# Top-k attention with a gated feed-forward: pairs of slots begin at slot 13, single blocks for x, two buffers for loaded q and k, values copied between the softmax's two functions

## The chip, the core and the metric

The kernel runs on one core of one Trainium2 chip. The metric is the device time of one execution in microseconds (us). The program works on five engines: TensorE (PE in the profile, its weight loads PEld), VectorE (DVE), ScalarE (ACT), GpSimd (POOL) and SyncE (SP), which issues nearly all DMA. Each engine takes its own instructions strictly in the order in which they are written.

## The reference

```python
# attention: q, k, v are (8, 8, 576, 64); top_k = 32
scores = scale * np.matmul(q, k.transpose(0, 1, 3, 2))
kth = np.partition(scores, -top_k, axis=-1)[..., -top_k:-top_k + 1]
scores = np.where(scores >= kth, scores, -1000000000.0)
attn = np.exp(scores - np.max(scores, axis=-1, keepdims=True))
attn = attn / (np.sum(attn, axis=-1, keepdims=True) + 1e-09)
x = np.matmul(attn, v)            # then (B,H,S,D) -> (B*S, H*D) = (4608, 512)
# feed-forward: w_in (512, 2048), w_out (2048, 512)
h = x @ w_in
g = h * (1.0 / (1.0 + np.exp(-1.702 * h)))
out = g @ w_out
```

Each row keeps the 32 largest of its 576 scores.

## The kernel before, in words

**Slots.** The unit of attention is a slot: 128 rows for two heads, thus 2 x 128 rows of 576 scores. A batch has four blocks of 128 rows and a tail of 64, times four pairs of heads: 16 full slots and two tail slots, 18 in all (`PER`), and 144 slots for the eight batches (`N`). In each batch the two tail slots are the 13th and 14th.

**What a slot goes through.** `scores` (PE, L282) fills PSUM, `copy_scores` (ACT, L294) brings it to SBUF. A top-k search on DVE finds the 32nd largest value. `exponentials` (ACT) runs two functions over the row: a Prelu that throws everything below the cut far down (L388) and an Exp whose sums fall out beside it (L391). The probabilities are transposed, and the values matmul (PE, L495 or L530) makes a 64-row piece of x for each head. When all four pairs of heads of a block are there, the block of x (128 tokens x 512) is put on the list `ready`. A quarter of the first feed-forward matmul for one block is `hidden` (L580, written H below), the quarter of the second is `project` (L628, P). A block takes four H and four P; there are 36 blocks, so 144 of each. Between them lie a tanh on ACT (L597, and a copy L600) and the gate on POOL (L609, L610), or on DVE in the first slots (L612).

**Two forms of slots.** Slots 0 to 11 (`SETTLED`) run one at a time in `slot(n)`. Their search (`topk`) runs over all 576 columns. The probabilities are transposed by PE matmuls against a diagonal matrix `by` with the inverse sums (L440, L443; `by` is made on POOL, L404, after `divide` on DVE has waited for the sums). From slot 12 on `two_slots(n)` runs slots n and n + 1 together. Its search (`topk_of_pairs`) first takes the greater and the lesser of column j and column j + 288: `pair_up` (DVE L323 for the greater, POOL L326 and L327 for the lesser), a slot ahead. It takes 32 values of the greater half and 16 of the lesser with MAX8 and MATCH_REPLACE8 over 288 columns (L337, L340), merges the two lists (L344) and takes the least (L347). The probabilities are transposed by DMA: `split` (ACT L462) separates the halves of each word, a DMA writes them to DRAM (L464), and a transposing DMA (L470) brings them back as `pt`. Inverse sums of a pair of slots are spread out on POOL (`wide`, L425), turned by PE (L519), copied with the values from PSUM to SBUF by ACT (`x`, L908), and multiplied on POOL into the block of x (`x_of`, L544).

**The order inside a pair.** The order is written by hand. For pair n: loads of slot n; bounds and `exponentials(n - 1)`, `split`; search n; H; P; tanh; `prepare_by_dma`; the turned sums of slots n - 3 and n - 2; scores n + 2 and their copy; values of n - 3 and n - 2; the transposing DMAs; scores n + 3; loads of slot n + 1; bounds and `exponentials(n)`; the copy `x` and `x_of`; `split(n)`; H; copy of scores n + 3; tanh; `prepare_by_dma` of slot n + 1; P; the copy of a finished output block (`ob`, L634); search n + 1. On PE this reads: H, P, turned sums, S(n + 2), values, S(n + 3), H, P.

**q and k of the next batch.** `load` (SP L184, L187: six DMAs for q and k of one pair of heads) fills `qk_l`, `prepare_by_dma` splits it (ACT L240, `halves`), writes it to DRAM (L244 to L249) and transposes it back (L253). Two tables say in which slot this happens, counted from the first slot of the batch: `FETCH` and `READY`, with tables of their own for batch 1 (`FETCH_1`, `READY_1`); `VALUES` does so for v.

**Buffers.** The pool `loads` has one buffer, `xtp` three of 128 x 4 x 2 x 128 (two blocks of x each), `ptp` and `prp` two each (`prp` holds the probabilities and `halves`), `ps_s` room for one slot's scores.

Of the kernel before, what the change touches and what calls it, by code (L numbers as in the profile page):

```python
# [9 lines left out]
ALU = mybir.AluOpType  # L10
ENG = mybir.EngineType
F32 = mybir.dt.float32
# [6 lines left out]
P = 128  # L19
TOPK = 32  # L20
# [10 lines left out]
def kernel(  # L31
# [27 lines left out]
    nc = tc.nc  # L59
# [9 lines left out]
    CC = C // P  # L69
# [12 lines left out]


    TURNS = 4
    SETTLED = 11
    assert D == 64 and 2 * TAIL == P and C == NP * P and C == PIECE and B % 2 == 0
    assert TOPK == 32 and NP == 4 and NF == 4 and NG == 4 and CC == 4

    const = ctx.enter_context(tc.tile_pool(name="const", bufs=1))
    pool = lambda name, bufs, **kw: ctx.enter_context(tc.tile_pool(name=name, bufs=bufs, **kw))  # L90
    raws = pool("raws", 8)
    loads = pool("loads", 1)
    vals = pool("vals", 4)
    qkt = pool("qkt", 6)
    scp = pool("scp", 4)
# [1 line left out]
    lefts = pool("lefts", 2)  # L97
    small = pool("small", 4)
    ptp = pool("ptp", 2)
    xtp = pool("xtp", 3)  # L100
    xtt = pool("xtt", 1)
    thp = pool("thp", 5)
    apart = pool("apart", 4, space=DRAM)
# [224 lines left out]

    def topk_of_pairs(n):

        top = st[n]["top"] = small.tile([P, 2, TOPK + TOPK // 2], F32, name="top2", tag="top")
        cut = st[n]["cut"] = small.tile([P, 2], F32, name="cut")
        first, few = greater.pop(n), lesser.pop(n)
        left = lefts.tile([P, 2, HALF], F32, name="left2", tag="left")

        def largest(src, r, i):
            nc.vector.max(top[:, i, 8 * r : 8 * r + 8], src[:, i, :])  # L337

        def remove(to, src, r, i):
            nc.vector.match_replace(to[:, i, :], top[:, i, 8 * r : 8 * r + 8], src[:, i, :], LOWEST)  # L340

        def merge():
            rest = top[:, :, TOPK // 2 : TOPK]
            nc.vector.tensor_tensor(out=rest, in0=rest, in1=top[:, :, : TOPK - 1 : -1], op=ALU.max)  # L344

        def bound():
            nc.vector.tensor_reduce(  # L347
                out=cut[:], in_=top[:, :, TOPK // 2 - 1 : TOPK], axis=mybir.AxisListType.X, op=ALU.min, negate=True
            )

        ops = []
        for r in range(TOPK // 8):
            ops += [lambda r=r, i=i: largest(left if r else first, r, i) for i in range(2)]
            if r < TOPK // 8 - 1:
                ops += [lambda r=r, i=i: remove(left, left if r else first, r, i) for i in range(2)]
        ops += [lambda: pair_up(n + 1) if n + 1 < N else None]
        for r in range(TOPK // 8, TOPK * 3 // 16):
            ops += [lambda r=r, i=i: largest(few, r, i) for i in range(2)]
            if r == TOPK // 8:
                ops += [lambda r=r, i=i: remove(few, few, r, i) for i in range(2)]  # L360
        return ops + [merge, bound]

    def lows(n):

        top, cut = st[n]["top"], st[n]["cut"]
        low = st[n]["low"] = small.tile([P, 2], F32, name="low")
        for i in range(2):
            nc.gpsimd.tensor_scalar(
                low[:, i : i + 1], cut[:, i : i + 1], top[:, i, 0:1], -1.0, op0=ALU.add, op1=ALU.mult
            )  # L370

    def bounds(n):

        if n > SETTLED:
            return lows(n)
        top = st[n]["top"]
        cut = st[n]["cut"] = small.tile([P, 2], F32, name="cut")
        low = st[n]["low"] = small.tile([P, 2], F32, name="low")
        nc.gpsimd.tensor_scalar(cut[:], top[:, :, TOPK - 1], -1.0, None, op0=ALU.mult)
        nc.gpsimd.tensor_tensor(out=low[:], in0=top[:, :, TOPK - 1], in1=top[:, :, 0], op=ALU.subtract)  # L380
# [15 lines left out]
    def divide(n):  # L396

        some = small.tile([P, 2], F32, name="some", tag="sums")
        nc.vector.tensor_scalar_add(some[:], st[n]["den"], 1e-9)
        rden = small.tile([P, 2], F32, name="rden", tag="inverse")  # L400
        nc.vector.reciprocal(rden[:], some[:])
        by = st[n]["by"] = xtt.tile([P, 2, P], F32, name="by", tag="xT_t")
        for i in range(2):
            nc.gpsimd.tensor_scalar(by[:, i, :], ident[:], rden[:, i : i + 1], None, op0=ALU.mult)  # L404

    sums = {}

    def sums_of(n):

        k = (n + 1) // 2  # L410
        if k not in sums:
            sums[k] = small.tile([P, 2, 2], F32, name="sums")
        return sums[k][:, (n + 1) % 2, :]

    def invert(n):

        k = (n + 1) // 2
        if k in sums:
            count = 2 if 2 * k < N else 1
            total = sums[k][:, 0:count, :]  # L420
            nc.vector.tensor_scalar_add(total, total, 1e-9)
            inverse = small.tile([P, 2 * count], F32, name="inverse")
            nc.vector.reciprocal(inverse[:], total.rearrange("p s j -> p (s j)"))
            wide = sums[k] = raws.tile([P, 2, 2, D], F32, name="wide", tag="raw")
            nc.gpsimd.tensor_copy(  # L425
                out=wide[:, 0:count, :, :].rearrange("p s j d -> p (s j) d"),
                in_=inverse[:].unsqueeze(2).to_broadcast([P, 2 * count, D]),
            )

    def turn(n, first, blocks):  # L430
# [43 lines left out]
    def x_at(b, t, hp):  # L474

        if t < NF:
            if (b, t // 2) not in xts:
                xts[b, t // 2] = xtp.tile([P, CC, 2, P], F32, name="xT")
            return xts[b, t // 2][:, hp, t % 2, :]
        if b // 2 not in xts:  # L480
            xts[b // 2] = xtt.tile([P, CC, P], F32, name="xT_t")
        return xts[b // 2][:, hp, b % 2 * TAIL : (b % 2 + 1) * TAIL]
# [33 lines left out]

    def sum_rows(m, to):

        nc.tensor.transpose(to, sums[(m + 1) // 2][:, (m + 1) % 2, :, :], ident[:])  # L519

    def values_at(m, o):

# [16 lines left out]
    def x_of(m, o, by):  # L539

        b, t, hps = slots[m]
        for p in range(2 if t == NF else 1):
            cols = slice(p * TAIL, (p + 1) * TAIL) if t == NF else slice(0, P)
            nc.gpsimd.tensor_tensor(out=x_at(b, t, hps[p]), in0=o[:, cols], in1=by[:, cols], op=ALU.mult)  # L544
        finish_x(m)

    def finish_x(m):

        b, t, hps = slots[m]
        if hps[-1] < NP - 1:  # L550
            return
        if t == NF:
            if b % 2:
                first = [(b - 1 + i) * S + FULL for i in range(2)]
                rows = [(slice(i * TAIL, (i + 1) * TAIL), out[x : x + TAIL, :]) for i, x in enumerate(first)]
                xT = xts.pop(b // 2)
                ready.append(([xT[:, c, :] for c in range(CC)], [rows]))
            return
        lines = out[b * S : b * S + FULL, :].rearrange("(p t) c -> p t c", t=NF)
        xT = xts[b, t // 2]  # L560
        ready.append(([xT[:, c, t % 2, :] for c in range(CC)], [[(slice(0, P), lines[:, t, :])]]))
        if t % 2:
            del xts[b, t // 2]

    ready = []
    hidden_at = {"f": 0}
# [87 lines left out]

    READY = (-12, -10, -4, -2)
    READY_1 = (-7, -4, -3, -2)
    FETCH = (-16, -11, -8, -3)
    FETCH_1 = (-12, -6, -3, -2)  # L660
    VALUES = (-1, 1, 1, 3)
    by_slot = dict(enumerate([2, 2, 3, 3, 3, 3, 3, 3, 3, 3, 2, 2]))
    for n in by_slot:
        first = sum(map(len, list(by_slot.values())[:n]))
# [95 lines left out]
    def slot(n):  # L760
# [11 lines left out]
        else:  # L772
# [10 lines left out]
            for piece in some:  # L783
                piece["size"]()
            tanh(False)
        for i, op in enumerate(topk(n)):
            op()
            if i == 2:
                for _ in range(min(3 if n >= TURNS else 6, len(unfinished))):
                    finish_one()  # L790
            if i == 5:
                if n > 0:
                    divide(n - 1)
                while unfinished:
                    finish_one()
            if i == 10:
                gate(False)
# [44 lines left out]
    def two_slots(n):  # L842
# [15 lines left out]
        def find(m):  # L858
            for i, op in enumerate(topk_of_pairs(m) if live(m) else [lambda: None] * 23):
                op()  # L860
                if i == 8 and m % 2 == 0:
                    invert(m - 2)
                if i > 1 and unfinished:
                    finish_one()
# [36 lines left out]
            scores(n + 3)  # L901
        begin(second)
        measure(n)
        if live(n):
            exponentials(n)
        if held:
            x = raws.tile([P, 2, 2, P], F32, name="x", tag="raw")
            nc.scalar.copy(out=x[:, 0 : len(held)], in_=o[:, 0 : len(held)])  # L908
            for i, m in enumerate(held):
                x_of(m, x[:, i, 1, :], x[:, i, 0, :])  # L910
        if live(n):
            split(n)
            turn_by_dma(n)
# [9 lines left out]
    with tc.manual_schedule():  # L923
        opening()
        for n in range(SETTLED + 1):
            slot(n)
        pair_up(SETTLED + 1)
        for n in range(SETTLED + 1, N + 4, 2):
            two_slots(n)
        while ready or to_gate or gated or to_project:  # L930
            last_slot()
# [30 lines left out]
```

## Time and profile before

| | us |
|---|---|
| median of 3 runs (lowest, highest) | 1510.85 (1510.18, 1513.99) |
| the profiled execution: time, span | 1512.53, 1510.7 |
| PE busy (share of the span) | 1443.9 (96%) |
| DVE busy | 1378.1 (91%) |
| ACT busy | 1171.7 (78%) |
| POOL busy | 891.1 (59%) |
| mean granted PE clock | 0.983 |

A row of a group gives the line, engine, operation, tiles and shapes, the count, and behind the bar the busy time in us and the mean of one in ns; then the engine's idle time ahead of these instructions and what ended it. A row of waits gives who waited for whom, the total in us, how often, and the longest. A row of the timeline gives start and duration in us, and in brackets the idle time before. Rows of windows give for each stretch its length and, for PE, PEld, DVE, ACT and POOL, the busy time with the count of instructions; then the PE clock, the DMA share and GB/s.

### The profile page before, as it was taken

To read this page: it belongs to the slowest core of one execution; us is meant where nothing else is said; L and a number is where in the kernel's file an instruction comes from. 1 tells how busy PE (TensorE), PEld (TensorE's weight loads), DVE (VectorE), ACT (ScalarE), POOL (GpSimd) and SP (SyncE) were. 2 spreads that over 40 slices of the span, in tenths; PEclk is the share of its full clock that TensorE was granted. 3 is DMA by queue.
4 is the path that set the end of the run, shared out by engine and by line. 5 is a ranking of instruction groups with operands and counts; after the bars stand their busy time and mean duration, and the time that the engine had idled before them with its cause. 6 is when DMAs were issued, how large, how long until landed. Compare 5 with 4: busy or idle time off the path is not lost. (4 is left out here: it accounts for less than half of the span.)

```text
span 1510.7 us, 31439 instructions
## 1 busy us (share of the span) xinstructions
PE 1443.9 (96%) x10729; PEld 1052.8 (70%) x10729; DVE 1378.1 (91%) x4542; ACT 1171.7 (78%) x1846; POOL 891.1 (59%) x1117
## 2 busy tenths in 40 slices
PE   6789878999999999999999999999999999999998
PEld 5667555767777777767777767777777777777775
DVE  7999989999999999999999999999999999999800
ACT  6998878878878787888878787888878888777720
POOL 3788645666666666666666556666666666656500
PEclk7899989999999999999999999999999999999999
DMA  7451876766858587666767667585776767444520
GB/s 226 134 156 43 196 198 184 190 174 171 188 158 211 149 201 194 159 182 157 210 160 182 167 178 191 159 199 150 196 194 155 192 161 207 140 129 134 133 55 14
DMA packets 533777, 248.35 MB, mean 164 GB/s; under 512 B 465136, under 2 KB 507888, under 8 KB 533616
## 3 DMA queue, kind: packets, MB, share of 16 engines
q1 hardware_dynamic: 533184, 246.05, 62.1%
q8 instruction: 84, 1.38, 0.4%
q14 instruction: 77, 0.63, 0.1%
q10 hardware_dynamic: 432, 0.30, 0.1%
HBM read 45.09 MB, written 105.32 MB: 100 GB/s over the span
## 5 line engine op out<-in xcount | busy, mean ns | idle before, releaser
L580 PEld LDWEIGHTS ph<-xT,win 128*128 128x128 f32 x4096 | 474.3, 192 | 69.7 <-issue 53.7
L628 PE MATMUL po<-wout,th 128*128 128x512 f32 x1152 | 518.5, 593 | 1.5 <-POOL wout L147 1.5
L580 PE MATMUL ph<-xT,win 128*128 128x128 f32 x4096 | 489.6, 277 | 12.0 <-POOL xT L544 12.0
L628 PEld LDWEIGHTS po<-wout,th 128*128 128x128 f32 x1152 | 208.1, 191 | 211.1 <-issue 207.9
L337 DVE MAX8 top<-left 128x8 f32<-128x288 f32 x792 | 325.6, 446 | 0.0
L462 ACT COPY sc<-pr 128x2304 uint16<-128x2304 uint16 x133 | 281.5, 2117 | 2.2
L294 ACT ACTIVATE sc<-s_ps 128x576 f32<-128x576 f32 x288 | 172.0, 653 | 128.9 <-PE s_ps L282 126.7
L544 POOL TENSOR_TENSOR xT<-x 128x128 f32<-128x128 f32 x117 | 51.4, 457 | 332.4 <-DVE top L344 161.3
L340 DVE MATCH_REPLACE8 left<-top,left 128x288 f32<-128x288 f32 x528 | 229.7, 443 | 0.0
L391 ACT ACTIVATE pr<-sc,low 128x576 f32<-128x576 f32 x288 | 220.9, 777 | 0.0
L337 DVE MAX8 top<-lesser 128x8 f32<-128x288 f32 x528 | 214.2, 447 | 0.0
L388 ACT ACTIVATE sc<-sc,cut 128x576 f32<-128x576 f32 x288 | 208.7, 783 | 1.6 <-DVE cut L347 1.3
L327 POOL TENSOR_TENSOR lesser<-lesser,greater 128x576 int32<-128x576 int32 x132 | 186.0, 1409 | 22.2 <-DVE greater L323 12.7
L282 PE MATMUL s_ps<-qk_t 64*128 64x288 f32 (+1 forms) x1280 | 186.3, 437 | 9.8 <-ACT sc L294 9.1
L326 POOL TENSOR_TENSOR lesser<-sc 128x576 int32<-128x576 int32 x132 | 187.5, 1421 | 0.0
L610 POOL TENSOR_TENSOR th<-th,h 128x512 f32<-128x512 f32 x127 | 161.7, 1273 | 10.6
L530 PE MATMUL o<-pt,v_l 128*64 128x128 f32 (+1 forms) x2384 | 146.2, 266 | 10.5 <-DMA pt<-rows 10.4
L530 PEld LDWEIGHTS o<-pt,v_l 128*64 128x64 f32 x2384 | 121.1, 138 | 38.6 <-issue 24.9
L597 ACT ACTIVATE th<-ph 128x512 f32<-128x512 f32 x144 | 86.5, 601 | 73.2 <-PE ph L580 73.0
L323 DVE TENSOR_TENSOR greater<-sc 128x576 f32<-128x576 f32 x132 | 104.4, 791 | 36.7 <-ACT sc L294 28.5
L282 PEld LDWEIGHTS s_ps<-qk_t 64*128 64x128 f32 (+1 forms) x1280 | 101.5, 180 | 51.3 <-issue 21.6
L609 POOL TENSOR_SCALAR th<-th 128x512 f32<-128x512 f32 x127 | 78.8, 620 | 66.2 <-ACT th L597 66.0
(86 smaller groups left out, 1648.0 us busy)
## 6 DMA issues: line engine op xcount, KB each, us to landing
rows<-sc SPq DMA_DIRECT2D x133, 576.0 KB, 3.2
qk_rows<-halves SPq DMA_DIRECT2D x56, 256.0 KB, 2.9
qk_l<-in_q_dram SPq DMA_DIRECT2D x64, 128.0 KB, 2.9
raw<-in_moe_w_in_dram SPq DMA_DIRECT2D x16, 512.0 KB, 5.1
v_l<-in_v_dram SPq DMA_DIRECT2D x32, 256.0 KB, 3.0
raw<-in_moe_w_out_dram SPq DMA_DIRECT2D x16, 512.0 KB, 3.7
out_dram<-ob SPq DMA_DIRECT2D x32, 256.0 KB, 2.9
qk_l<-in_k_dram SPq DMA_DIRECT2D x62, 128.0 KB, 2.9
```

What stands on the lines that cost most here:

```text
L282: nc.tensor.matmul(ps[i][rows, c, 0:HALF], lhsT=qT[b, hps[p]][on, cols], rhs=kT[b, hps[p]][on, FIRST[i] + c * HALF : FIRST[i] + (c + 1) * ...
L294: nc.scalar.mul(out=to, in_=ps[i][:, :, 0:HALF], mul=SCALE)
L326: nc.gpsimd.tensor_tensor(out=whole, in0=a.bitcast(I32), in1=b.bitcast(I32), op=ALU.add)
L327: nc.gpsimd.tensor_tensor(out=whole, in0=whole, in1=greater[n][:].bitcast(I32), op=ALU.subtract)
L337: nc.vector.max(top[:, i, 8 * r : 8 * r + 8], src[:, i, :])
L340: nc.vector.match_replace(to[:, i, :], top[:, i, 8 * r : 8 * r + 8], src[:, i, :], LOWEST)
L388: nc.scalar.activation(sc[:, i, :], sc[:, i, :], AF.Prelu, bias=cut[:, i : i + 1], alpha=HUGE)
L391: nc.scalar.activation(pr[:, i * S : (i + 1) * S], sc[:, i, :], AF.Exp, bias=low[:, i : i + 1], accum_out=den[:, i : i + 1],)
L462: nc.scalar.copy(out=halves, in_=pr[:].bitcast(U16).rearrange("p (k h) -> p h k", h=2))
L530: nc.tensor.matmul(o[j * D : (j + 1) * D, cols], lhsT=main[:, j, c, :] if c < NF else tail[:, j, :], rhs=pt[:, MAIN[j] + c if c < NF else ...
L580: nc.tensor.matmul(ph[:, i * tiles * P : (i + 1) * tiles * P], lhsT=win[:, c, f * P : (f + 1) * P], rhs=xT[c], start=(c == 0), stop=(c == ...
L628: nc.tensor.matmul(po[:], lhsT=gT[:, i * P : (i + 1) * P], rhs=wout[:, f, :], start=(f == 0), stop=(f == FC - 1))
```

## The change

Five things change. (1) Slot 12 runs in the single form, with the search over pairs of columns; `two_slots` begins at slot 13, so all pairs are (odd, even). There are 68 pairs before and after. The tables of loads move to odd slots, so that in the steady part all of `FETCH` and `READY` fall on the first slot of a pair. (2) `loads` has two buffers. (3) `xtp` has four buffers of one block each instead of three of two blocks. (4) The copy `x` and `x_of` move between the Prelu and the Exp of `exponentials(n)`. (5) In the search, two MAX8 results of the lesser half are written backwards beside the others, and the merge becomes one TENSOR_REDUCE over pairs instead of a TENSOR_TENSOR that reads one operand backwards. Besides, `by` is made with two operations (times the inverse, times 1) instead of one.

```diff
-    SETTLED = 11
+    SETTLED = 12
+    PAIRED = 12
...
-    loads = pool("loads", 1)
+    loads = pool("loads", 2)
...
-    xtp = pool("xtp", 3)
+    xtp = pool("xtp", 4)
...
-        top = st[n]["top"] = small.tile([P, 2, TOPK + TOPK // 2], F32, name="top2", tag="top")
+        top = st[n]["top"] = small.tile([P, 2, 2 * TOPK], F32, name="top2", tag="top")
...
+        def found(r, i, written=False):
+            if r < TOPK // 8:
+                at = (8 * r + TOPK) % (TOPK + TOPK // 2)
+                return top[:, i, at : at + 8]
+            end = 2 * TOPK - 8 * (r - TOPK // 8) - TOPK
+            return top[:, i, end - 1 : end - 9 : -1] if written else top[:, i, end - 8 : end]
+
         def largest(src, r, i):
-            nc.vector.max(top[:, i, 8 * r : 8 * r + 8], src[:, i, :])
+            nc.vector.max(found(r, i, True), src[:, i, :])
...
         def merge():
-            rest = top[:, :, TOPK // 2 : TOPK]
-            nc.vector.tensor_tensor(out=rest, in0=rest, in1=top[:, :, : TOPK - 1 : -1], op=ALU.max)
+            both = top[:, :, 0:TOPK].rearrange("p i (s k) -> p i k s", s=2)
+            nc.vector.tensor_reduce(
+                out=top[:, :, TOPK + TOPK // 2 :], in_=both, axis=mybir.AxisListType.X, op=ALU.max
+            )
...
-            nc.gpsimd.tensor_scalar(by[:, i, :], ident[:], rden[:, i : i + 1], None, op0=ALU.mult)
+            nc.gpsimd.tensor_scalar(by[:, i, :], ident[:], rden[:, i : i + 1], 1.0, op0=ALU.mult, op1=ALU.mult)
...
-            if (b, t // 2) not in xts:
-                xts[b, t // 2] = xtp.tile([P, CC, 2, P], F32, name="xT")
-            return xts[b, t // 2][:, hp, t % 2, :]
+            if (b, t) not in xts:
+                xts[b, t] = xtp.tile([P, CC, P], F32, name="xT")
+            return xts[b, t][:, hp, :]
...
-    READY = (-12, -10, -4, -2)
-    READY_1 = (-7, -4, -3, -2)
-    FETCH = (-16, -11, -8, -3)
-    FETCH_1 = (-12, -6, -3, -2)
-    VALUES = (-1, 1, 1, 3)
+    READY = (-13, -11, -5, -3)
+    READY_1 = (-5, -4, -3, -1)
+    FETCH = (-17, -15, -9, -7)
+    FETCH_1 = (-11, -9, -3, -1)
+    VALUES = (0, 1, 2, 3)
...
-        for i, op in enumerate(topk(n)):
+        for i, op in enumerate(topk_of_pairs(n) if n >= PAIRED else topk(n)):
...
-        if live(n):
-            exponentials(n)
-        if held:
+        def bring():
+            if not held:
+                return
             x = raws.tile([P, 2, 2, P], F32, name="x", tag="raw")
-            nc.scalar.copy(out=x[:, 0 : len(held)], in_=o[:, 0 : len(held)])
+            nc.scalar.copy(out=x[:], in_=o[:])
             for i, m in enumerate(held):
                 x_of(m, x[:, i, 1, :], x[:, i, 0, :])
+
+        if live(n):
+            exponentials(n, bring)
+        else:
+            bring()
...
         for n in range(SETTLED + 1):
+            if n == PAIRED:
+                pair_up(n)
             slot(n)
-        pair_up(SETTLED + 1)
         for n in range(SETTLED + 1, N + 4, 2):
             two_slots(n)
```

The indices of the inverse sums follow the new parity (`(n + 1) // 2` becomes `n // 2`), so that both slots of each pair share a tile.

More of the change, by code (lines that the diff above doesn't have):

```diff
@@ L334, in topk_of_pairs @@
         left = lefts.tile([P, 2, HALF], F32, name="left2", tag="left")
+        def found(r, i, written=False):
[4 more added lines that the diff above has]
+            return top[:, i, end - 1 : end - 9 : -1] if written else top[:, i, end - 8 : end]
         def largest(src, r, i):
-            nc.vector.max(top[:, i, 8 * r : 8 * r + 8], src[:, i, :])
+            nc.vector.max(found(r, i, True), src[:, i, :])
         def remove(to, src, r, i):
-            nc.vector.match_replace(to[:, i, :], top[:, i, 8 * r : 8 * r + 8], src[:, i, :], LOWEST)
+            nc.vector.match_replace(to[:, i, :], found(r, i), src[:, i, :], LOWEST)
         def merge():
-            rest = top[:, :, TOPK // 2 : TOPK]
-            nc.vector.tensor_tensor(out=rest, in0=rest, in1=top[:, :, : TOPK - 1 : -1], op=ALU.max)
+            both = top[:, :, 0:TOPK].rearrange("p i (s k) -> p i k s", s=2)
+            nc.vector.tensor_reduce(
+                out=top[:, :, TOPK + TOPK // 2 :], in_=both, axis=mybir.AxisListType.X, op=ALU.max
+            )
         def bound():
             nc.vector.tensor_reduce(
-                out=cut[:], in_=top[:, :, TOPK // 2 - 1 : TOPK], axis=mybir.AxisListType.X, op=ALU.min, negate=True
+                out=cut[:], in_=top[:, :, TOPK + TOPK // 2 - 1 :], axis=mybir.AxisListType.X, op=ALU.min, negate=True
             )
@@ L368, in lows @@
             nc.gpsimd.tensor_scalar(
-                low[:, i : i + 1], cut[:, i : i + 1], top[:, i, 0:1], -1.0, op0=ALU.add, op1=ALU.mult
+                low[:, i : i + 1], cut[:, i : i + 1], top[:, i, TOPK : TOPK + 1], -1.0, op0=ALU.add, op1=ALU.mult
             )
     def bounds(n):
-        if n > SETTLED:
+        if n >= PAIRED:
             return lows(n)
@@ L403, in divide @@
         for i in range(2):
-            nc.gpsimd.tensor_scalar(by[:, i, :], ident[:], rden[:, i : i + 1], None, op0=ALU.mult)
+            nc.gpsimd.tensor_scalar(by[:, i, :], ident[:], rden[:, i : i + 1], 1.0, op0=ALU.mult, op1=ALU.mult)
     sums = {}
     def sums_of(n):
-        k = (n + 1) // 2
+        k = n // 2
         if k not in sums:
             sums[k] = small.tile([P, 2, 2], F32, name="sums")
-        return sums[k][:, (n + 1) % 2, :]
+        return sums[k][:, n % 2, :]
     def invert(n):
-        k = (n + 1) // 2
+        k = n // 2
         if k in sums:
-            count = 2 if 2 * k < N else 1
-            total = sums[k][:, 0:count, :]
+            total = sums[k][:]
             nc.vector.tensor_scalar_add(total, total, 1e-9)
-            inverse = small.tile([P, 2 * count], F32, name="inverse")
+            inverse = small.tile([P, 4], F32, name="inverse")
             nc.vector.reciprocal(inverse[:], total.rearrange("p s j -> p (s j)"))
@@ L425, in invert @@
             nc.gpsimd.tensor_copy(
-                out=wide[:, 0:count, :, :].rearrange("p s j d -> p (s j) d"),
-                in_=inverse[:].unsqueeze(2).to_broadcast([P, 2 * count, D]),
+                out=wide[:].rearrange("p s j d -> p (s j) d"),
+                in_=inverse[:].unsqueeze(2).to_broadcast([P, 4, D]),
             )
@@ L517, in sum_rows @@
     def sum_rows(m, to):
-        nc.tensor.transpose(to, sums[(m + 1) // 2][:, (m + 1) % 2, :, :], ident[:])
+        nc.tensor.transpose(to, sums[m // 2][:, m % 2, :, :], ident[:])
     def values_at(m, o):
@@ L559, in finish_x @@
         lines = out[b * S : b * S + FULL, :].rearrange("(p t) c -> p t c", t=NF)
[L560 to L563, printed above, removed]
+        xT = xts.pop((b, t))
+        ready.append(([xT[:, c, :] for c in range(CC)], [[(slice(0, P), lines[:, t, :])]]))
     ready = []
@@ L860, in find @@
                 op()
-                if i == 8 and m % 2 == 0:
+                if i == 8 and m % 2:
                     invert(m - 2)
```

## The prediction

> **What bounds the kernel now.** I read the page first (PE is busy for 96% of the span, DVE for 91%), then the busy time by stage, because an average over stages hides which engine is last. The four stretches are: slots 0 to 11; the first pairs up to the turned sums of pair 22; the steady part; the drain.
>
> ```profile
> 0.00:152.00 152.00, 125.16 (x985) 101.58 (x986) 139.93 (x320) 129.84 (x260) 105.31 (x119) 0.89 0.45 139
> 152.00:257.30 105.30, 86.10 (x562) 56.73 (x561) 97.34 (x335) 82.10 (x122) 56.70 (x72) 0.92 0.76 196
> 257.30:1459.60 1202.30, 1185.39 (x8917) 861.38 (x8916) 1136.66 (x3883) 954.76 (x1457) 728.65 (x927) 1.00 0.66 171
> 1459.60:1510.70 51.10, 47.21 (x270) 33.07 (x268) 4.13 (x6) 5.04 (x9) 0.45 (x1) 0.99 0.04 11
> ```
>
> The first number after the length is PE's busy time. PE idles 26.8 us in the first stretch, 19.2 in the second, 16.9 in 1202 in the third, 3.9 in the drain: 66.8 us in all. In the third stretch PE is the bound, and the change removes no matmul. So all that can be won is PE's idle time, and I asked the waits what it is made of.
>
> ```profile
> PE ph L580 <- POOL xT L544: 12.0, 16, 0.9
> PE o L530 <- DMA pt<-rows: 10.4, 7, 3.6
> PE s_ps L282 <- ACT sc L294: 9.1, 2, 8.4
> ...
> ACT halves L240 <- DMA qk_l<-in_k_dram: 11.5, 3, 6.0
> ```
>
> Sixteen times H waits for the last piece of its block of x; seven times the values wait for the transposed probabilities; once scores wait 8.4 us for ACT, which had waited itself for loaded q and k. What a wait on x looks like:
>
> ```profile
> 1369.35 1.44 ACT L388 ACTIVATE sc<-sc,cut 128x576 f32<-128x576 f32 x2
> ...
> 1372.20 0.57 ACT L908 COPY x<-o 128x512 f32<-128x512 f32 x1
> ...
> 1372.85 0.87 POOL L544 TENSOR_TENSOR xT<-x 128x128 f32<-128x128 f32 x2 [6.35 <-DVE top L344]
> ...
> 1371.62 0.94 PE L580 MATMUL ph<-xT,win 128*128 128x128 f32 x6
> 1373.36 3.17 PE L580 MATMUL ph<-xT,win 128*128 128x128 f32 x26 [0.80 <-POOL xT L544]
> ```
>
> The values were finished at 1370.5. ACT runs both Exps first and copies them at 1372.20, POOL multiplies, and H stops after three of the first four matmuls. The pair with such a wait lasts 20.1 us by its turned sums (1366.71 to 1386.81), the next, without, 19.1 (to 1405.91).
>
> **The copy between Prelu and Exp.** An Exp pair with its sums lasts 1.5 us (1370.68 to 1372.20). Moved ahead of it, the copy can start when the Prelu ends or the values are done, whichever is later: about 0.1 us after the values. Copy 0.5, a step of 0.1 and two products of 0.44 put the block 1.5 us after the values' end. H begins 1.1 us after it (1371.62) and reaches its fourth part 0.7 us later, at 1.8. The wait goes, with 0.3 us to spare. Next late is nothing: PE simply runs on. Fifteen of the 16 waits lie behind 257 us; they hold 11 us of idle time, and by the length of pairs (20.1 against 19.1) they cost up to 15. I take 12. The Exps and `split` of that slot move back by about 0.5 us where ACT waits for the values; behind them stand the score copy, the tanh and the rows for the transposing DMA. ACT is 78% busy and waits 3.7 and 1.8 us for scores in those two pairs, so that costs nothing unless that slack is gone.
>
> **Loads on the first slot of a pair, two buffers.** A load holds SP for 3.9 us (184.38 to 188.3). Where `FETCH` falls on the second slot (-11 and -3), it stands on SP ahead of that slot's rows and their transpose, which the values need one pair later. All positions become first ones, and no pair of the steady part has both a load and a prepare. The three waits of values behind 257 us (1.47, 1.19, 2.84) sum to 5.5; I take 4. The buffers themselves cost nothing: a load comes four slots ahead of its use. In batch 1, however, loads and prepares of heads 2 and 3 share slots 15 and 17; that is in the next part.
>
> **Slot 12 alone, and the first pairs.** From pair 21 after, and pair 22 before, the program has the same number of H, P and pairs left (63 pairs), plus one set of scores (1.2 us) and one of values (1.5): 2.7 us more after. So I compare the start of the turned sums of pair 21 with 257.3. I walk the engines' orders with durations of this stretch: Prelu pair 1.3, Exp pair 1.5, `split` and `halves` 2.0 each, score copy 1.1, tanh and copy 1.0, H and P 3.5, scores 1.2, values 1.5, search 9.0, load 3.9 on SP and 1.9 more to its landing, rows 3.2, transposing DMA 2.6 to 3.0 on SP and 2 more.
>
> Slot 12 begins on DVE at 147.8 as before. `halves` no longer stands ahead of `exponentials(11)`, which runs from 150.5 to 153.4; `divide` waits for it, the search ends at 161. PE has been idle since 152 when `by` comes at 155; transposes (new on PE, 2.3 us), scores, values, P, H end at 167. The output copy `ob` stands on ACT ahead of `exponentials(12)` until 164, the block's last copy comes at 169.1 and H waits 2 us for it. Scores 15 are copied at 177.6 (DVE wants them at 176). `halves` of slot 14 ends at 186.6, its four writes leave SP at 190.7, only then goes the load of slot 15 and lands at 196.5: ACT, free at 192.5, waits 4.0, and DVE waits 4.0 for scores 17. Behind `halves` of slot 15 SP has 2.3 of writes, 2.6 and 6 of transposes; rows 15 go at 209.5, their transpose ends at 215.3, the load of slot 17 lands at 221.7: ACT, free at 212.4, waits 9.3. Scores 19 are copied at 224.8, DVE loses 7, PE about 6. Two P, turned sums and scores 21 end at 234.7, the transposed probabilities of slot 17 land at 240.4, values and scores end at 243.1, two H and two P at 257.1. That is 0.2 us ahead of 257.3. The gain of the shift (one slot's search less before this point, and no `halves` at slot 11) is spent on the two waits for loads. I count 0, with 6 us to either side, and 10 on the good side if SP is quicker than walked.
>
> **The search.** One rule of the Trainium skill speaks against the new merge. The row first:
>
> ```profile
> L344 DVE TENSOR_TENSOR top<-top x132: 191/194/1282, 157.3 to 1430.2; 128x32 f32<-128x32 f32 x132
> L347 DVE TENSOR_REDUCE cut<-top 128x2 f32<-128x34 f32 x132 | 25.0, 190 | 4.5
> ```
>
> Minimum, median and maximum: the old merge takes 0.19 us, or up to 1.28 us when POOL is at work; its mean is 484 ns. "VectorE: DVE Perf Modes", section "Rules for kernel authors", calls `tensor_reduce` the slowest operation of the engine and advises against it on a hot path. The reduce row here takes 190 ns for 34 elements. If I let the rule stand and scale it with the 64 elements, the new merge takes 0.36 us, a gain of 0.12 x 132 = 16 us of DVE time; by the row as it is, 0.29 x 132 = 39. The measured row decides: small operations here cost a fixed amount. "SBUF — State Buffer", section "Who interferes with whom", says that a DVE instruction with two SBUF inputs contends with a GpSimd one that reads SBUF and that `tensor_reduce` does not; the spread of L344 agrees. Either gain is DVE time in a stage that PE bounds, so its worth for the end is 0 now; in the first pairs, where DVE waits for scores, it hides too. No MAX8 of before writes backwards. The nearest row is the old merge, which reads backwards in 191 ns at its shortest, no more than the forward reduce: 0 extra. The other end is a rival below; below nothing is excluded, since the forward MAX8 does the same work.
>
> **At no cost.** Single blocks of x: at most three live at a time (one being written, one waiting, one read by H), so four suffice; were that cover gone, POOL would wait for an H of 3.5 us. `by` in two operations: 605 ns for 128 columns in one operation, 620 ns for 512 in two (L609), so perhaps 0.3 us less each in slots 1 to 12, where DVE is full (139.9 of 152): 0. If it gained nothing, nothing changes.
>
> **The sum**, against the profiled execution: span 1510.7 - 12 (x) - 4 (transposes) - 0 (first pairs) + 2.7 (work moved behind that point) = 1497.4. The drain has six H and seven P behind the last values in both orders, and PE is full there: 0. The profiled time is 1512.5, 1.8 more than its span, and itself 1.7 above the median of 1510.85. Taken from the median, 13.3 less is 1497.5; I say 1497.
>
> **The rivals.** (a) The first pairs gain: if the load of slot 17 lands early enough, 10 of the 19.2 us of idle go as well: 1487. For it speaks that before, the two load waits of 6.0 and 5.0 cost PE 8.4 and a colder clock (0.76); against it, that slot 17 has fetch and prepare together. Chance 0.24. (b) As summed: 0.52. (c) Hidden anyway: H no longer waits for x, but the Exps behind the copy come late, their rows and transposes with them, and the values wait instead: the 16 us return but for a few. For it, seven such waits exist; against it, the slack of 1.8 to 3.7 on ACT: 1508. Chance 0.14. (d) Slower: the backward MAX8. There are eight in a pair. DVE is busy for 17.8 and 19.7 us in the two pairs quoted, 18.7 on average; less 0.6 for the merge, 18.1 of 19.1. From 0.12 us extra for each on, DVE becomes the bound. At 0.2 us each the pair lasts 19.7, 0.6 x 66 = 40 us, so 1537. Against it speaks the old merge. Chance 0.07; another 0.03 for the first pairs failing by more than 15.
>
> **How the numbers follow.** A difference under 0.3% (4.5 us) can't be told from none. (a) and (b) are faster but for a tail of (b): 0.77, and a little of (c): 0.79. The rest of (c) and of (b): 0.12. Slower: 0.09. The range reaches from the full gain of (a) with 15 for x, 1482, to just beyond (c), 1509.
>
> **What would show it.** After: no PE wait on POOL's xT of any size behind 257 us; all steady pairs near 19.1 us; ACT's wait for `qk_l` twice, some 4 and 9 us, near 195 and 215; L344's successor near 0.2 us without spread; MAX8 into `top` from the lesser half still 447 ns. I am wrong if the turned sums of pair 21 start well away from 257, or if waits on `pt<-rows` grow.

## The result, and the profile after

| | before | after |
|---|---|---|
| median of 4 runs each (lowest, highest), us | 1512.42 (1510.18, 1515.26) | 1505.01 (1503.92, 1506.61) |
| profiled execution: time, span | 1512.53, 1510.7 | 1505.19, 1503.4 |
| PE, DVE, ACT, POOL busy | 1443.9, 1378.1, 1171.7, 891.1 | 1446.8, 1381.6, 1176.5, 858.1 |

The ratio is 0.9951 with a 95% interval of 0.9929 to 0.9973. The kernel is faster, by 7.4 us where 13.3 were forecast. The sum had the right sign and two wrong terms in it (the first pairs and the transposed probabilities), which the stretches show. Below are the windows of the kernel after, cut at the turned sums of pair 21 (268.6 us) and at the last ones. After the length come PE's, PEld's, DVE's, ACT's and POOL's busy time, then the clock.

```profile
152.00:268.60 116.60, 91.58 (x550) 61.29 (x551) 92.34 (x322) 73.84 (x107) 49.84 (x66) 0.87 0.58 149
268.60:1450.53 1181.93, 1181.93 (x8925) 860.79 (x8924) 1145.87 (x3894) 965.96 (x1467) 704.36 (x931) 1.00 0.68 176
1450.53:1503.40 52.87, 48.39 (x291) 34.30 (x289) 4.13 (x6) 5.36 (x9) 0.87 (x2) 1.00 0.04 11
```

PE is busy for all of the 1181.9 us of the steady part: not one wait is left. That part was 1202.3 long, so 20.4 us went, with 16 - 1.2 expected (the scores moved behind the cut lie here, the values moved lie in the drain, which grew by 1.8). But the cut itself comes at 268.6 where it was to come at 257.1: 11.3 us later than the 257.3 of before. The prediction had named this as its sign of being wrong. 11.3 - 20.4 + 1.8 = -7.3, the difference of the spans.

What became of the wait for x. A pair of the kernel after whose H needs a fresh block (timeline; start, duration, and in brackets the idle time before):

```profile
329.00 1.04 PE L539 MATMUL o<-pt,v_l 128*64 128x128 f32 x16
329.87 0.39 PE L539 MATMUL o<-pt,v_e 128*64 128x128 f32 x4
...
330.37 0.58 ACT L915 COPY x<-o 128x512 f32<-128x512 f32 x1
...
331.02 0.87 POOL L553 TENSOR_TENSOR xT<-x 128x128 f32<-128x128 f32 x2 [4.16 <-ACT x L915]
...
331.32 3.84 PE L587 MATMUL ph<-xT,win 128*128 128x128 f32 x32
```

The values end at 330.3, the copy starts 0.1 us later, the block is there at 331.9, and H runs through its 32 records (matmul entries of the trace) in 3.84 us without a stop; before it stopped after six.

Where the first pairs lost time. PE's waits and those of ACT that stand behind them, in the kernel after:

```profile
161.99 0.83 PE L587 MATMUL ph<-xT,win 128*128 128x128 f32 x6
167.99 5.32 PE L587 MATMUL ph<-xT,win 128*128 128x128 f32 x26 [5.17 <-ACT xT L517]
174.48 3.84 PE L587 MATMUL ph<-xT,win 128*128 128x128 f32 x32 [1.16 <-ACT h L607]
...
181.68 1.24 PE L283 MATMUL s_ps<-qk_t 64*128 64x288 f32 x8
...
226.05 1.09 PE L539 MATMUL o<-pt,v_l 128*64 128x128 f32 x16 [3.75 <-DMA pt<-rows]
...
233.54 2.83 PE L283 MATMUL s_ps<-qk_t 64*128 64x288 f32 x8 [6.11 <-ACT sc L295]
...
250.46 1.45 PE L539 MATMUL o<-pt,v_l 128*64 128x128 f32 x16 [3.87 <-DMA pt<-rows]
```

```profile
162.19 0.60 ACT L641 ACTIVATE ob<-po 128x512 f32<-128x512 f32 x1 [3.69 <-PE po L635]
...
167.68 0.26 ACT L517 COPY xT<-o 128x128 f32<-128x128 f32 x1
...
204.25 2.11 ACT L241 COPY halves<-qk_l 128x2304 uint16<-128x2304 uint16 x1 [5.10 <-DMA qk_l<-in_k_dram]
...
230.83 2.11 ACT L241 COPY halves<-qk_l 128x2304 uint16<-128x2304 uint16 x1 [9.93 <-DMA qk_l<-in_k_dram]
```

The two load waits came nearly as walked (4.0 and 9.3 forecast). The first H of slot 11's block did not: it stopped for 5.2 us instead of 2, its 26 records then took 5.32 us where the same 26 take 3.17 in the steady part, and a second H followed, after a further wait of 1.2 us for ACT's copy `h`. Only then come the scores of slot 15 (181.68). The walk's times leave room for the rest of one H and a P between the copy and these scores.

And the opening. SP's queue, before and then after (the load of head pair 2); the row of waits between them is what SP waited for before, PE's transposes (L694) that read the one buffer:

```profile
13.01 1.24 SPq L184 DMA_DIRECT2D qk_l<-in_q_dram  x2
```

```profile
SPq L184 <- PE tp L694: 5.2, 1, 5.2
```

```profile
7.78 1.23 SPq L185 DMA_DIRECT2D qk_l<-in_q_dram  x2
```

Slot 12 starts on DVE at 144.8 after and at 147.8 before. So from slot 12's start to the cut it is 109.5 us before and 123.8 after: the first pairs lose 14.3, and the opening gives back 3.1.

### The profile page after: what moved, and what is told of

Its sections match the earlier page's. It is cut to its first block, busy times and chain, and to the rows that moved or that the text cites. A ratio compares the mean times of both kernels' runs of the same rounds, so it can differ in the third digit from the quotient of the medians.

```text
span 1503.4 us, 31378 instructions
## 1 busy us (share of the span) xinstructions
PE 1446.8 (96%) x10748; PEld 1057.4 (70%) x10748; DVE 1381.6 (92%) x4541; ACT 1176.5 (78%) x1849; POOL 858.1 (57%) x1119
## 4 chain that ended last, share of the span: by engine, by line
PE 85%; DMA 0%; SPq 0%; ACT 0%; issue 0%; ACTq 0%
PE ph L587 32%; PE po L635 32%; PE o L539 10%; PE s_ps L283 10%; PE o L528 1%; DMA pt<-rows 0%; DMA qk_l<-in_k_dram 0%; SPq L185 0%; ACT halves L241 0%; SPq L479 0%; ACT ob L641 0%; SPq L188 0%; SPq L643 0%; ACT sc L295 0%; ACTq L241 0%
## 5 line engine op out<-in xcount | busy, mean ns | idle before, releaser
L327 POOL TENSOR_TENSOR lesser<-sc 128x576 int32<-128x576 int32 x132 | 186.9, 1416 | 8.2 <-ACT sc L295 8.2
L324 DVE TENSOR_TENSOR greater<-sc 128x576 f32<-128x576 f32 x132 | 139.8, 1059 | 31.8 <-ACT sc L295 25.7
```

The source lines that it names most:

```text
L327: nc.gpsimd.tensor_tensor(out=whole, in0=a.bitcast(I32), in1=b.bitcast(I32), op=ALU.add)
```

## The experiments

All ratios are against the kernel before, run on the same chip; the kernel before had medians of 1512 to 1517 us on these chips, so times from different chips are not subtracted. "The cut" is the start of the turned sums of pair 21 (22 in kernels with the old parity) in the profile, "steady" the stretch from there to the last turned sums.

**1. The last copy of slot 11's block earlier on ACT.**

```diff
-            values(n - 1, put_off)
+            values(n - 1, None if n == SETTLED else put_off)
```

> The changed kernel with the last copy of the first-form blocks (slot 11) placed on ScalarE ahead of the output copy, the exponentials and the split of slot 12; TensorE's order is the same. Theory A (the loss of the first pairs is largely H waiting for that copy): the 5.2 us wait of H goes, the cold matmuls behind it too (5.3 us for 26 records), turned sums of pair 21 some 8 us earlier, near 260, time near 1497. Theory B (the loss is the single slot itself, and the waits only show it): idle moves to the next wait, less than 2 us gained.

Measured: 1501.42 us, 0.9911 (0.9888 to 0.9933); the cut at 263.8, 4.8 earlier; steady 1181.5. The wait of 5.2 is gone, but H now stops once for 3.1 us, for PSUM that ACT has not emptied yet (its copy `h`), and behind that stop its 32 records take 5.46 us instead of the 3.73 of the H ahead of it:

```profile
161.46 3.73 PE L587 MATMUL ph<-xT,win 128*128 128x128 f32 x32
168.27 5.46 PE L587 MATMUL ph<-xT,win 128*128 128x128 f32 x32 [3.07 <-ACT h L607]
```

So the gain is 4.8 of the 8 us that theory A said. B is out.

**2. Batch 1's loads of heads 2 and 3 at slots 14 and 15.**

```diff
-    FETCH_1 = (-11, -9, -3, -1)
+    FETCH_1 = (-11, -9, -4, -3)
```

> The changed kernel with the loads of heads 2 and 3 of batch 1 at slots 14 and 15 instead of 15 and 17. Theory A (ScalarE's waits for loaded q and k hold up scores, and these VectorE and TensorE): both waits of ScalarE (5.1 and 9.9 us) go, TensorE's waits of 3.4 and 6.1 us for score copies and 3.8 and 3.9 us for transposed probabilities shrink; 8 to 12 us gained, near 1495. Theory B: SyncE is the limit, the wait moves to the rows and transposes behind the earlier load, less than 3 us gained.

Measured: 1494.94 us, 0.9871 (0.9848 to 0.9894); the cut at 259.7, 8.9 earlier. ACT no longer waits for loads at all, the waits of 3.4 and 6.1 us for scores are gone; the two waits for transposed probabilities do not shrink, as theory A had it, but grow from 7.6 us together to 9.9. Theory A, at its lower end by the cut.

**3. Both edits.**

> Both edits of the two runs before. Theory A: they add, 16 to 20 us gained, near 1487, turned sums of pair 21 near 249. Theory B: less than the larger of the two plus 2 us.

Measured: 1491.49 us, 0.9843 (0.982 to 0.9865); the cut at 255.3, 13.3 earlier (4.8 and 8.9 make 13.7). They add, though to less than the 16 to 20 us expected. From slot 12's start that is 110.8 us, close to the 109.3 of my walk, but this does not show that the walk's error lay in these two places: the walk had the two load waits in it, and this kernel has none. With the copy alone put right (experiment 1) the stretch is 119.4 us, still 10.1 longer than walked.

**4. The copy x behind the Exps again.**

```diff
-        if live(n):
-            exponentials(n, bring)
-        else:
-            bring()
+        if live(n):
+            exponentials(n)
+        bring()
```

> The changed kernel with the copy x and its products behind the Exps again, as before the change. Theory A (the move removed the waits of H for the last piece of x): about 15 steady pairs last 20.1 us again, 12 to 15 us slower, near 1518. Theory C (the parity alone did it: heads 2 and 3 of a block now come in one pair, and loads no longer share a pair with prepares): at most 3 us slower.

Measured: 1526.92 us, 1.0081 (1.006 to 1.0103): without the move the new parity is slower than before. Fifteen steady pairs last 20.5 us and more, steady is 1205.6. This is the wait in the waits view, first of this kernel, then of the kernel before:

```profile
PE ph L587 <- POOL xT L553: 15.4, 15, 1.8
```

```profile
PE ph L580 <- POOL xT L544: 12.0, 16, 0.9
```

Theory A had the mechanism; its size was too small. A pair costs 1.4 us instead of 1.0. In the new parity heads 2 and 3 of a block come in the same pair: H stops after four records instead of six, and its last piece needs both products on POOL (0.44 us each) instead of the first alone, which fits the 0.4 us.

**5. The move alone, in the kernel before.**

> The kernel before with only the copy x and its products moved between Prelu and Exp. Theory A (H waits for x because the copy stands behind two Exps): the 15 pairs of 20.1 us behind the turned sums of pair 22 become 19.1, the few waits for transposed probabilities stay; 12 to 16 us faster than before. Rival (the Exps then come late and the values wait for their transposes): under 5 us faster, more waits on pt.

Its edit is the last hunk but one of the change's diff (the function `bring`; the copy itself stays as it was). Measured: 1501.84 us, 0.9907 (0.9879 to 0.9935), with single runs from 1497.5 to 1512.4; the cut at 257.8, steady 1188.9 instead of 1202.3, so 13.4 us between one profiled execution of each. No wait of H for xT is left behind the cut, and the 15 pairs of 20.1 us last 19.0 to 19.2; the waits for transposes are nearly as before (10.4 us, 7 waits):

```profile
PE o L530 <- DMA pt<-rows: 11.1, 9, 3.0
```

Theory A. The move alone gains as much as the whole change, or more (the intervals overlap).

**6. Two load buffers alone, in the kernel before.**

```diff
-    loads = pool("loads", 1)
+    loads = pool("loads", 2)
...
-    xtp = pool("xtp", 3)
+    xtp = pool("xtp", 4)
```

with single blocks of x.

> The kernel before with two buffers for loaded q and k (and x in four single blocks, which makes the room); tables of loads unchanged. Theory A (in the opening the load of head pair 2 no longer waits on SyncE for the buffer of pair 0, and the first weights follow earlier): slot 3 starts some 2.7 us earlier, 2 to 4 us faster, steady part unchanged. Rival (the earlier opening of the changed kernel was chance): no difference, slot 3 starts near 43.9 us.

Measured: 1513.38 us, 0.9976 (0.9962 to 0.999). Slot 3 starts at 41.4 us (43.9 before), slot 12 at 145.4. Theory A: 4.0 us by the medians on one chip, 3.6 by the ratio. The 16 runs spread from 1507.7 to 1518.0; the profiled one (1516.48) lies above their median, with a steady part 6.4 us longer than in the profile of before, 3.1 us of it in waits for transposed probabilities.

**7. The old lists and merge in the changed kernel** (forward MAX8 results, TENSOR_TENSOR as in the first lines of the diff's `merge`).

> The changed kernel with the old search lists: forward results, and the merge as a two-operand TENSOR_TENSOR that reads one list backwards. Theory A (VectorE's time is hidden under TensorE in the steady part): within 2 us of the changed kernel, although VectorE is busy some 20 to 40 us more. Rival (the merge shortens the search on the path): 5 to 15 us slower.

Measured: 1511.33 us, 0.996 (0.9947 to 0.9973), on another chip than the changed kernel's first runs, whose interval overlaps. But its steady part had 15 pairs of 19.5 us, so I ran both on one chip.

> The changed kernel itself once more, for a comparison on one chip with the next run. Both theories: 0.995 of the kernel before, turned sums of pair 21 near 268, no steady pair above 19.7 us.

> The changed kernel with the old lists and the two-operand merge once more, on one chip with the run before. Theory D (the longer merge shifts VectorE's two-operand pair_up so that it starts just ahead of the products of x on GpSimd, which then wait about 0.5 us for it): the pairs whose H needs a fresh block last 19.5 instead of 19.1 us, some 6 us slower than the changed kernel. Theory A (VectorE's time is hidden, and the first comparison only differed by chance): within 2 us of the run before.

Measured: the changed kernel 1505.79 us, 0.994 (0.9927 to 0.9953); with the old merge 1511.35 us, 0.9973 (0.9963 to 0.9983). The old merge costs 5.6 us; steady is 1188.0 against 1181.5, again with 15 pairs above 19.35. Theory D. One such pair with the old merge, timeline:

```profile
330.01 0.74 DVE L324 TENSOR_TENSOR greater<-sc 128x576 f32<-128x576 f32 x1
...
330.13 1.34 POOL L544 TENSOR_TENSOR xT<-x 128x128 f32<-128x128 f32 x2 [2.96 <-ACT x L906]
...
330.43 4.27 PE L578 MATMUL ph<-xT,win 128*128 128x128 f32 x32
```

and the changed kernel at the same place:

```profile
329.26 0.74 DVE L324 TENSOR_TENSOR greater<-sc 128x576 f32<-128x576 f32 x1
...
330.58 0.87 POOL L553 TENSOR_TENSOR xT<-x 128x128 f32<-128x128 f32 x2 [4.16 <-ACT x L915]
...
330.88 3.84 PE L587 MATMUL ph<-xT,win 128*128 128x128 f32 x32
```

With the old merge `greater` starts 0.1 us ahead of the products of x, which then last 1.34 us instead of 0.87, and H is 0.4 us longer: 15 x 0.4 = 6 us. With the new one `greater` is over when the products begin. In the old parity the collision is not there: the kernel of experiment 5 has the old merge too, but in it the products begin first (283.06 us, `greater` at 284.01) and last 0.87 us, and the 15 pairs last 19.0 to 19.2.

**8. The copy x early only from pair 19 on, with both edits of experiment 3.**

```diff
-            exponentials(n, bring)
-        else:
+            exponentials(n, bring if n > 17 else lambda: None)
+        if n <= 17 or not live(n):
             bring()
```

> Both edits of the first pairs (earlier copy, earlier loads) and, for pairs 13 to 17 only, the copy x behind the Exps. Theory A (in the first pairs the values wait for transposed probabilities, ScalarE waits for the values ahead of its Exps, and so the next transposes come late): ScalarE's two waits of 4.5 us leave its path, turned sums of pair 21 some 3 to 5 us earlier, near 251, time near 1487. Rival (SyncE's order decides, not ScalarE): no gain over the kernel with both edits.

Measured: 1492.63 us, 0.9837 (0.9823 to 0.985); the cut at 255.5, no earlier than 255.3. PE's two waits for transposed probabilities are still there (9.9 us, 8.7 in experiment 3). The rival holds: it is not ACT's order that makes those transposes late.

**9. Steady loads on the second slot of a pair.**

```diff
-    FETCH = (-17, -15, -9, -7)
+    FETCH = (-16, -14, -8, -6)
```

> The changed kernel with the steady loads on the second slot of a pair (16, 14, 8 and 6 slots ahead of the batch instead of 17, 15, 9 and 7). Theory A (such a load stands on SyncE ahead of that slot's rows, and the values then wait for the transposes): waits on pt behind the first pairs come back, 4 to 10 us slower than the changed kernel. Rival (the transposes have slack in the new parity): within 2 us.

Measured: 1504.62 us, 0.9933 (0.992 to 0.9946), beside 0.994 of the changed kernel on the same chip; steady 1181.9. The rival holds: the second slot as such costs nothing.

**10. Batch 1's loads and prepares spread, with the edit of experiment 1.**

```diff
-    READY_1 = (-5, -4, -3, -1)
-    FETCH_1 = (-11, -9, -3, -1)
+    READY_1 = (-7, -5, -3, -1)
+    FETCH_1 = (-11, -9, -6, -4)
```

> The changed kernel with the earlier copy of slot 11's block and batch 1's loads and prepares spread: loads at slots 7, 9, 12 and 14, prepares at 11, 13, 15 and 17, so that pairs 13 and 15 no longer carry three prepares and a load in a row. Theory E (SyncE's queue of writes and two transposes of q and k delays the transposed probabilities of slots 15 and 17): the two waits of values of about 4.4 us left in the kernel with both edits go, turned sums of pair 21 near 248, some 5 to 8 us faster than that kernel, near 0.980 of the kernel before. Rival: the waits move elsewhere, no faster than 0.984.

Measured: 1486.95 us, 0.9813 (0.9797 to 0.9829); the cut at 250.6. That is 4.8 us earlier than with both edits, just under the 5 to 8 expected. Of PE's two waits for transposed probabilities, first in the kernel with both edits, one is left:

```profile
PE o L539 <- DMA pt<-rows: 8.7, 2, 4.5
```

```profile
PE o L539 <- DMA pt<-rows: 1.9, 1, 1.9
```

A new one of 2.7 us, for POOL's `wide`, stands beside it. Theory E. This version beats both kernels: 1.9% below the kernel before, 1.3% below the changed one on the same chip (1505.79).

## Why the forecast was wrong in size, point by point

| term of the sum | forecast | measured | from |
|---|---|---|---|
| copy between Prelu and Exp | -12 | -13.4 | experiment 5, steady part |
| transposed probabilities | -4 | -8.2 | not measured alone: the rest of the steady part, 20.4 + 1.2 - 13.4 |
| work moved behind the cut | +2.7 | +3.0 | 1.2 taken as forecast, 1.8 in the drain |
| first pairs and opening | 0 | +11.3 | the cut, 268.6 against 257.3 |
| sum | -13.3 | -7.3 | |

**The step that failed is the walk of "Slot 12 alone, and the first pairs"**, the term that was counted as 0 and came out at 11.3 us. It had set "the block's last copy comes at 169.1 and H waits 2 us for it". By the walk's durations (score copy 1.1, scores 1.2) the scores of slot 15 start at 175.3, 27.5 us after slot 12's start; they came 36.9 us after it. That is 9.4 of the 14.5 us by which the walk was short (123.8 against 109.3), and it is made up as follows. The copy ended 23.2 us after slot 12's start instead of 21.3 (1.9). From there the walk leaves 6.2 us, for the rest of one H (2.7) and a P (3.5); it took 13.7. The rest of H ran at a lower clock (granted clock 0.58 from 167.9 to 173.4 us) and took 5.32 us instead of 2.7 (2.6), PE then waited for ACT's copy `h` (1.2), and a second H stood ahead of the P (3.7). The other 5.1 us lie between those scores and the cut and are not taken apart. Experiment 1 gets 4.8 us back with PE's order unchanged, so the position of one small copy on ACT, behind `ob`, the Exps and `split`, is shown as a cause. The two load waits of 4.0 and 9.3 us had been walked nearly right (5.1 and 9.9), and experiment 2 shows their worth, 8.9 us: I had counted them, but as used up by a gain of the shift that did not come.

**Smaller slips.** The 0.76 that rival (a) calls a clock stands in the row shown as the DMA share; the clock there is 0.92. The chances of (a) and (b) sum to 0.76, not 0.77, and those of slower to 0.10, not 0.09. The opening, taken "as before", came 3.1 us earlier.

**The copy x: right, and bigger in its place.** 13.4 us by itself, 24 in the new parity (1205.6 against 1181.5). That the Exps "move back by about 0.5 us" at no cost is right for the whole change: behind the cut PE has no wait at all. With the move alone (experiment 5) six waits of 6.4 us for transposes stand in the steady part, where before had four of 5.7; one execution of each does not tell whether the later Exps make that difference.

**Loads on first slots: the number came, the reason did not.** The waits on transposes vanished from the steady part, and the term gave 4.2 us more than forecast, without which the gain would have been 3.1 us. But experiment 9 puts the loads on second slots and they stay away. They are also away with the copy x late (experiment 4), and they stay in the old parity with the copy x early (experiment 5). What is left as a reason is the new tables and parity, in which no steady pair holds both a load and a prepare; parity and sharing were not tried apart, so the cause stays open. That part of the gain was luck.

**"The buffers themselves cost nothing"** missed a gain. The second buffer frees SP's queue in the opening by 5.2 us, slots start 2.7 to 3 us earlier from slot 3 on, and experiment 6 shows it (2.4 to 2.5 us there).

**"Its worth for the end is 0"**, of the merge, was wrong by 5.6 us in the changed kernel (experiment 7). It is no gain over the kernel before, whose order has no such collision, but a loss that the new parity would have brought. The row's duration was nearly right: L352 takes 222 ns for 64 elements, between the row (190) and the scaled rule (360), and nearer the row. That DVE time is hidden is right too: DVE is no less busy than before (1381.6 us), since `greater` now takes more:

```profile
L352 DVE TENSOR_REDUCE top<-top 128x32 f32<-128x64 f32 x132 | 29.2, 222 | 4.5
L324 DVE TENSOR_TENSOR greater<-sc 128x576 f32<-128x576 f32 x132 | 140.2, 1062 | 30.7 <-ACT sc L295 24.4
```

(the changed kernel of experiment 7; 791 ns before). What I left out is that a two-operand instruction on DVE can hold up POOL, and that POOL's products of x lie on PE's path. The Trainium skill ("SBUF — State Buffer", section "Who interferes with whom") says that it is the order of issue that decides which of the two is held up; I had read it for DVE's time alone. The timelines of experiment 7 agree and show it in the direction that costs: `greater` first, POOL's products done in 1.34 us instead of 0.87.

The backward MAX8 (rival d) costs nothing: 445 ns for the lesser half, 447 before.

## What to carry to other kernels

Before a shift of a software pipeline is counted as free, walk its seam with every H, copy and queue in its written order: a 0.26 us copy behind an output copy, the exponentials and a `split` on another engine stopped the bounding engine for 5.2 us, and the lower clock after the stop added 2.2 us. A buffer or a shorter instruction that is "hidden" must be asked once more who else it lets start, on its queue (a second buffer in the opening) and at a port (a merge whose length decides whether GpSimd or VectorE comes first). Where one part of a change carries the gain, measure it alone: here moving one copy between two functions gained 0.9%, as much as all five parts together (0.5 to 0.6%) or more.

## What the runs showed of the hardware that was not expected

- GpSimd's TENSOR_SCALAR with two operations over 128 x 128 took 370 to 377 ns where the form with one operation took 601 to 615 (`by`, after and before).
- Two products of 128 x 128 on GpSimd took 1.34 us instead of 0.87 when a two-operand VectorE instruction had started 0.1 us before them (old merge, experiment 7, at 330.0 us), and the same VectorE instruction took 1.42 us instead of 0.74 when a two-operand instruction of GpSimd (L327) had started 0.6 us before it (changed kernel of experiment 7, at 319.7 and 329.3 us).
- After a stop of 5.2 us TensorE needed 5.32 us for 26 records that take 3.17 in the steady part. The granted clock of that stretch (167.9 to 173.4 us) was 0.58, against 1.00 in the steady part, and 5.32 x 0.58 = 3.1. After a stop of 3.1 us (experiment 1) 32 records took 5.46 us instead of 3.73, at a granted clock of 0.70 (168.2 to 173.8 us).
